# Windowed attention and a highway layer on one core: a fill in another order, earlier first completions, and a tail shared out anew between VectorE and GpSimd

## The chip, the cores and the metric

The kernel runs on one core of a Trainium2 chip. The metric is the device time of one execution in microseconds. It was 115.84 us before the change, the median of three runs from 115.61 to 115.97. PE stands for TensorE, DVE for VectorE, ACT for ScalarE, POOL for GpSimd and SP for SyncE, as in the profile.

## The reference

Attention with 4 sink keys and a window of 128 is followed by a gated layer on the result. The sizes are 4 batches, 8 heads, 768 positions, 64 elements per head, so 3072 rows of 512.

```python
scores = scale * np.matmul(q, k.transpose(0, 1, 3, 2))
keep = is_sink | in_window          # key < 4, or 0 <= query - key < 128
scores = np.where(keep, scores, -1000000000.0)
a = np.exp(scores - max); a = a / (sum + 1e-09)
x = np.matmul(a, v)                 # heads side by side: 3072 x 512
H = np.maximum(x @ w_h, 0.0)
T = 1.0 / (1.0 + np.exp(-(x @ w_t + b_t)))
out = T * H + (1.0 - T) * x
```

## The kernel before

The rows are cut into N = 24 tiles of 128 queries, NC = 6 per batch. The loop at L471 goes over steps n = 0 to 25. In step n PE computes the scores of tile n (`scores`, L265: mask matmuls L272, then L279 on the transposed q and k), the weighted values of tile n - 1 (`values`, L330, with the sink matmuls L311 and L317 of `starts` ahead of them), and the two products of the highway layer for tile n - 2 (`gate`, L369, and `hidden`, L387). Between these it transposes the attention result X of tile n - 1 (`x_transpose`, L359), which the next step's products need. In the profile a step starts with the eight L272 matmuls.

Each engine works through its own queue in the order in which the program is written; `_keep_traced_order` (L24) ties every instruction to the one ahead of it on its engine. So the order of the calls in the loop is the schedule, and lists ahead of the loop (L430 to L455) say at which step a transposition, a load or a completion comes.

**q and k** come from memory through POOL's queue, 32 partitions per load (`load_part`, L105), cast to 16 bits on the way into the tiles `nat`. DVE turns them into `tr` (`transpose_qk`, L118, the instruction L125). Batches 0 and 1 are split into three segments of 256 positions, batches 2 and 3 into two of 384. The scores of tile 3 are the first to need the third segment's q of batch 0, those of tile 4 the first to need its k. `loads` (L442) says how many loads POOL issues per step for batches 1 to 3. At most eight of POOL's loads are under way: before the next, the profile shows POOL waiting for the landing of an earlier one.

**V** comes through SP's queue (`load_v`, L129; `v_at`, L446, names the step), in steps 0 to 5 only after that step's scores. `cast_v` (L141) makes it 16 bits wide, on DVE for tiles 0 to 4 and on POOL from tile 5 on (`LATE` = 5). The outputs leave through SP's queue too, so a V load stands behind the outputs of the steps before.

**X.** ACT exponentiates the scores (`expo`, L323). When the values are in PSUM, DVE takes reciprocals of the row sums (L349) and writes X (L351): `norm`, L346. ACT copies the transposed X out of PSUM (L367) and computes tanh of the gate's product (L378, tile `TH`).

**Completion.** sigmoid(z) is 0.5 tanh(z/2) + 0.5. `diff` (L400, instruction L403) gives max(H, 0) - X in `DD`, on DVE. `complete(m)` (L423) then does three things for tile m: `gate_value` (L380, instruction L384) turns TH into 0.5 TH + 0.5, `gated` (L407, L408) multiplies DD by it on DVE, and `finish` (L411, L414) adds X and sends the sum out. Tile N - 2 takes its gate from ACT and its sum from DVE; all other sums are POOL's. Gates of tiles 12 to 20 are POOL's as well (`POOL_GATES`, L73), the others DVE's. `completed` (L449) completes tile n - 6 in step n up to step 20, and two tiles in each of the steps 21 to 24. `ahead` (L452) has the gates of tiles 15 to 20 computed on POOL earlier in the queue. The last tile is done in two halves behind the loop (L550 to L562).

DVE's queue in one step, in the middle of the run, is therefore: L349 and L351 for tile n - 1, one or two transpositions, L403 for tile n - 2, then L384 and L408 for the tile that is completed.

Of the kernel before, what the change touches and what calls it, by code (L numbers as in the profile page):

```python
# [11 lines left out]
FP32 = mybir.dt.float32  # L12
BF16 = mybir.dt.bfloat16
AF = mybir.ActivationFunctionType
ALU = mybir.AluOpType
# [22 lines left out]
def kernel(  # L38
# [13 lines left out]
    P = 128  # L52
    pe, act, dve, pool, sp = nc.tensor, nc.scalar, nc.vector, nc.gpsimd, nc.sync
# [7 lines left out]
    NT, DM = out.shape  # L61
    assert NT == B * S and DM == H * D
    NC = S // P
    N = B * NC
# [5 lines left out]
    SCALE = 1.0 / math.sqrt(D)  # L70

    LATE = 5
    POOL_GATES = range(12, 21)  # L73

    const = ctx.enter_context(tc.tile_pool(name="const", bufs=1))
    data = ctx.enter_context(tc.tile_pool(name="data", bufs=1))
    work = ctx.enter_context(tc.tile_pool(name="work", bufs=4))
# [40 lines left out]
    def transpose_qk(b, i, which, hgs=slice(0, HG)):  # L118

        t0, nt = segments[b][i]  # L120
        run = nt // 32
        src = nat[b][i][:, which, hgs].bitcast(FP32).rearrange("p hg m i -> p hg m i")
        dst = tr[b][:, which, hgs].bitcast(FP32).rearrange("p hg t e -> p hg (t e)")[
            :, :, t0:t0 + nt].rearrange("p hg (r m) -> p hg m r", m=run)
        dve.transpose(out=dst, in_=src)  # L125
# [73 lines left out]
    for g in range(1, G):  # L199
        m = away[32 * g:32 * g + 32, :]  # L200
# [5 lines left out]
                      op0=ALU.add, op1=ALU.max)  # L206
    dve.tensor_scalar(out=powers[:, 0], in0=powers[:, 0], scalar1=-1.0, scalar2=-3.0 * P,
                      op0=ALU.mult, op1=ALU.max)
    dve.tensor_scalar(out=powers[:, 1], in0=away, scalar1=-3.0, scalar2=0.0,
                      op0=ALU.add, op1=ALU.min)  # L210
    dve.tensor_scalar(out=powers[:, 2], in0=away, scalar1=0.0, scalar2=3.0,
                      op0=ALU.max, op1=ALU.min)
    dve.tensor_scalar(out=powers[:, 3], in0=powers[:, 2], scalar1=-1.0, scalar2=3.0,
                      op0=ALU.mult, op1=ALU.add)
    dve.tensor_scalar(out=inside, in0=away, scalar1=0.0, scalar2=-_OUT,
                      op0=ALU.is_ge, op1=ALU.mult)
# [127 lines left out]
    X = [None] * N  # L344

    def norm(n):  # L346
        rec = work.tile([P, HG, G], FP32, tag="rec", name="rec")
        av = ps_av[:, :, 0:G * (D + 1)].rearrange("p hg (g e) -> p hg g e", e=D + 1)
        dve.reciprocal(out=rec, in_=av[:, :, :, D])  # L349
        X[n] = work.tile([P, HG, G, D], FP16, tag="X", name="X", bufs=10)  # L350
        dve.tensor_tensor(out=X[n], in0=av[:, :, :, 0:D],  # L351
                          in1=rec.unsqueeze(3).to_broadcast([P, HG, G, D]), op=ALU.mult)
# [24 lines left out]
        TH[n] = work.tile([P, DM], FP16, tag="TH", name="TH", bufs=8)  # L377
        act.activation(out=TH[n], in_=ps_z, func=AF.Tanh, scale=0.5)  # L378

    def gate_value(n):  # L380
        if n == N - 2:
            act.activation(out=TH[n], in_=TH[n], func=AF.Copy, scale=0.5, bias=0.5)
        else:
            (pool if n in POOL_GATES else dve).tensor_scalar(  # L384
                out=TH[n], in0=TH[n], scalar1=0.5, scalar2=0.5, op0=ALU.mult, op1=ALU.add)

    def hidden(n, kcs=range(KC), cols=slice(0, DM), into=None):  # L387
# [9 lines left out]
    def flat(x, cols):  # L397
        return x.rearrange("p hg g d -> p (hg g d)")[:, cols]
# [19 lines left out]
    def idle(count):  # L418
        for _ in range(count):
            pe.matmul(ps_h, lhsT=zeros[:, 0:P], rhs=zeros, start=True, stop=True,  # L420
                      skip_group_check=True)

    def complete(m):  # L423
        if not any(m in ms for ms in ahead.values()):
            gate_value(m)
        gated(m)
        finish(m, eng=dve if m == N - 2 else pool)
# [12 lines left out]
    issues = [(b, i, g, which) for b in range(1, B) for i in range(len(segments[b]))  # L440
              for which in range(2) for g in range(G)][2 * G:]
    loads = {}  # L442
    for n, count in zip(range(2, 17), [4] * 4 + [3, 3, 3, 3, 2, 3, 3, 3, 3, 3, 3]):
        loads[n] = [issues.pop(0) for _ in range(count)]
    assert not issues
    v_at = {0: (2,), 1: (3, 4), 2: (5,), 3: (6,), 4: (7,), 5: (8,), 6: (9,), 7: (10, 11)}  # L446
    for n in range(8, N):
        v_at[n] = (n + 4,)
    completed = {n: (n - 6,) for n in range(6, 21)}  # L449
    completed.update({21: (15, 16), 22: (17, 18), 23: (19, 20), 24: (21, 22)})  # L450

    ahead = {18: (15,), 19: (16, 17), 20: (18,), 21: (19,), 22: (20,)}  # L452
    sinks_at = {2: (0, (2, 3)), 4: (0, (4, 5))}
    for b in range(1, B):
        sinks_at[b * NC + 2] = (b, (2, 3, 4, 5))  # L455
# [15 lines left out]
    for n in range(N + 2):  # L471

        nb, n1 = n - 2, n - 1
        if n < N:
            after = scores(n)
            expo(n)
            for m in v_at.get(n, ()):
                if m < N:
                    load_v(m, after if n < 6 else None)
            if n % NC == 3 and n // NC + 1 < B:  # L480
                load_sinks(n // NC + 1)
        if 4 <= n <= 6:
            hidden(n - 4 if n < 6 else 3)
        if n == 0:
            idle(5)
        starts(n1 if 0 <= n1 < N else None, nb if nb >= 0 else None)
        if 0 <= n1 < N:
            values(n1)
        if LATE <= n < N:
            cast_v(n, pool)  # L490
        if n == 2:
            sink_values(0)
            load_rows(1, 0, 0)
            load_rows(1, 0, 1)
        for b, i, g, which in loads.get(n, ()):
            load_part(b, i, g, which)
        if NC <= n < N and n % NC == 0:
            sink_values(n // NC)
        if NC <= n < N and n % NC == 1:
            sink_keys(n // NC)  # L500

        if 4 <= n <= 6:
            diff(n - 4 if n < 6 else 3)
        if n == 3:
            transpose_qk(0, 2, 1)
        turn = list(units.get(n, ()))
        if n == 5:
            transpose_qk(*turn.pop(0))
        if 0 <= n1 < N:
            norm(n1)  # L510
        if n == 1:
            transpose_qk(0, 1, 1)
        if 0 < n < LATE:
            cast_v(n, dve)
        if n == 1:
            transpose_qk(0, 2, 0)
        for unit in turn:
            transpose_qk(*unit)

        if nb >= 0:  # L520
            gate(nb)
            tanh(nb)
        if n == 5:
            hidden(2)
        if n == 1:
            idle(3)
        if 6 <= n <= N:
            hidden(nb, range(KC // 2))
        if 0 <= n1 < N:
            x_transpose(n1)  # L530
            if n in sinks_at:
                sink_scores(*sinks_at[n])
            x_copy(n1)
            if n in sinks_at:
                sink_expo(*sinks_at[n])
        if 6 <= n <= N:
            hidden(nb, range(KC // 2, KC))
        done = completed.get(n, ())
        for m in ahead.get(n, ()):
            gate_value(m)  # L540
        for m in done[:-1]:
            complete(m)
        if n == 5:
            diff(2)
        if 6 <= n <= N:
            diff(nb)
        for m in done[-1:]:
            complete(m)
# [2 lines left out]
    h_right = ps_av[:, 0, 0:DM // 2]  # L551
    hidden(last, cols=left)
    hidden(last, cols=right, into=h_right)
    O[last] = work.tile([P, DM], FP32, tag="O", name="O")
    for cols, h in ((left, None), (right, h_right)):
        diff(last, cols, h)
        dve.scalar_tensor_tensor(out=DD[last][:, cols], in0=TH[last][:, cols], scalar=1.0,
                                 in1=DD[last][:, cols], op0=ALU.add, op1=ALU.mult)
    for cols, engine in ((left, sp), (right, act)):
        dve.scalar_tensor_tensor(out=O[last][:, cols], in0=DD[last][:, cols], scalar=0.5,  # L560
                                 in1=flat(X[last], cols), op0=ALU.mult, op1=ALU.add)
        engine.dma_start(out=out[last * P:, cols], in_=O[last][:, cols])  # L562

    _keep_traced_order(tc)
# [33 lines left out]
```

## Time and profile before

| what | value |
|---|---|
| median of three runs | 115.84 us (115.61 to 115.97) |
| the profiled execution | 115.46 us, of which the span is 113.6 us |
| busy, of the span | PE 86%, PEld 46%, DVE 76%, ACT 67%, POOL 79% |
| mean granted clock of PE | 0.969 |
| chain that ended last, by engine | PE 27%, DMA 24%, DVE 19%, POOL 14% |
| DMA | 20.82 MB in 36705 packets, mean 183 GB/s |

The profile holds one execution. The span runs from the first to the last instruction; what is left up to the execution's own time lies around it. "Busy" is the time in which an engine had an instruction under way; times of instructions are given in us from the span's start. A line of the timeline gives the start, the duration, the engine and line, the tiles written and read with their shapes, and, in brackets, how long the engine had been idle and what released it. PEld are PE's weight loads, which overlap its matmuls. Matmul ends are modelled, and spans on POOL are rough.

### The profile page before, as it was taken

The page shows a single profiled execution, that of the slowest core. Times are in us where ns is not written, and L with a number is a line of the kernel's source. Part 1 is how long each engine was busy: PE and PEld are TensorE (multiplying, and loading weights), DVE is VectorE, ACT ScalarE, POOL GpSimd, SP SyncE. Part 2 cuts the span into 40 slices and gives each one's busy share as a digit, 9 for nine tenths or more (in the row PEclk, how much of TensorE's full clock was granted, in tenths as well). Part 3 has the DMA queues.
Part 4 walks back from the last instruction along what each step waited for, and adds up shares of the span by engine and source line. Part 5 has one row for each costly group of instructions (what it writes and reads, how often), then busy time and mean ns, then how long its engine had stood idle before and what let it go on. Part 6 is the DMA issues. An engine that isn't in the chain of part 4 may idle for free.

```text
span 113.6 us, 3578 instructions
## 1 busy us (share of the span) xinstructions
PE 98.3 (86%) x1414; PEld 51.8 (46%) x1414; DVE 86.2 (76%) x180; ACT 76.0 (67%) x94; POOL 90.1 (79%) x146
## 2 busy tenths in 40 slices
PE   5956773999989999999999999999979799998800
PEld 2413441644535545655465555665535366534400
DVE  6778827346394999798988978899856778899960
ACT  4476772947846588698777898785886587852500
POOL 6997549839699599999599999995989887997400
PEclk9999999769999999999999999999999999999985
DMA  3999999999999729999999999999955122424431
GB/s 87 224 234 218 175 213 247 203 218 235 187 238 151 106 71 193 253 244 223 208 247 213 198 207 243 215 197 239 287 142 151 47 85 92 185 104 179 156 149 66
DMA packets 36705, 20.82 MB, mean 183 GB/s; under 512 B 27340, under 2 KB 33232, under 8 KB 36688
## 3 DMA queue, kind: packets, MB, share of 16 engines
q1 hardware_dynamic: 29536, 13.37, 44.9%
q0 software_dynamic: 6848, 6.82, 38.0%
q10 hardware_dynamic: 304, 0.39, 1.2%
q8 instruction: 11, 0.18, 0.6%
q14 instruction: 6, 0.05, 0.2%
HBM read 21.11 MB, written 6.29 MB: 241 GB/s over the span
## 4 chain that ended last, share of the span: by engine, by line
PE 27%; DMA 24%; DVE 19%; POOL 14%; issue 7%; SPq 4%; DVEq 1%; POOLq 0%
DMA nat<-in_k_dram 7%; DMA wt<-in_moe_w_t_dram 7%; PE ps_h L390 7%; DMA wh<-in_moe_w_h_dram 7%; POOL nat L109 6%; DVE tr L125 5%; PE ps_z L371 5%; DVE DD L403 4%; DMA V<-in_v_dram 4%; PE ps_s L279 4%; DVE X L351 3%; DVE DD L408 3%; POOL TH L384 3%; PE ps_av L338 2%; SPq L174 2%
## 5 line engine op out<-in xcount | busy, mean ns | idle before, releaser
L327 ACT ACTIVATE E<-ps_s,ebias 128x2048 f16<-128x2048 f32 (+1 forms) x24 | 43.8, 1825 | 12.6 <-PE ps_s L279 12.6
L414 POOL TENSOR_TENSOR O<-DD,X 128x512 f32<-128x512 f16 x22 | 25.5, 1162 | 7.9 <-DVE DD L408 4.1
L125 DVE STREAM_TRANSPOSE tr<-nat 128x384 f32<-128x384 f32 (+1 forms) x28 | 26.1, 960 | 5.0 <-DMA nat<-in_q_dram 2.5
L390 PE MATMUL ps_h<-wh,XT 128*128 128x512 f16 (+1 forms) x96 | 27.4, 375 | 0.0
L109 POOL DMA_DIRECT2D nat<-in_k_dram x40 | 22.0, 557 | 6.1 <-DMA wt<-in_moe_w_t_dram 2.4
L371 PE MATMUL ps_z<-wt,XT 128*128 128x512 f16 x96 | 25.5, 389 | 0.0
L403 DVE SCALAR_TENSOR_TENSOR DD<-ps_h,X 128x512 f16<-128x512 f32 (+1 forms) x24 | 16.2, 674 | 8.7 <-PE ps_h L390 8.7
L378 ACT ACTIVATE TH<-ps_z 128x512 f16<-128x512 f32 x24 | 14.2, 593 | 8.4 <-PE ps_z L371 7.9
L367 ACT COPY XT<-ps_av 128x512 f16<-128x512 f16 x24 | 14.1, 586 | 6.8 <-PE ps_av L293 4.1
L109 POOL DMA_DIRECT2D nat<-in_q_dram x32 | 17.4, 551 | 1.1 <-DMA nat<-in_k_dram 1.1
L351 DVE TENSOR_TENSOR X<-ps_av,rec 128x512 f16<-128x512 f32 x24 | 16.6, 691 | 0.9
L408 DVE TENSOR_TENSOR DD<-DD,TH 128x512 f16<-128x512 f16 x23 | 13.7, 597 | 3.1 <-POOL TH L384 2.5
L279 PE MATMUL ps_s<-tr 32*128 32x256 f16 (+1 forms) x384 | 14.1, 261 | 1.9 <-DVE tr L125 1.9
L341 PE MATMUL ps_av<-v,E 128*128 128x65 f16 x192 | 14.5, 196 | 0.3 <-DVE v L142 0.2
L362 PE MATMUL ps_av<-ident,X 128*128 128x128 f16 x96 | 9.6, 224 | 4.5 <-DVE X L351 4.4
L338 PE MATMUL ps_av<-v,E 128*128 128x65 f16 x160 | 13.0, 197 | 0.0
L338 PEld LDWEIGHTS <-E 128*128 128x128 f16 x160 | 10.5, 99 | 5.5 <-issue 5.5
L341 PEld LDWEIGHTS <-E 128*128 128x128 f16 x192 | 12.1, 99 | 1.3 <-issue 1.3
L362 PEld LDWEIGHTS <-X 128*128 128x128 f16 x96 | 5.8, 99 | 14.1 <-DVE X L351 14.1
L142 POOL CAST v<-V 128x512 f16<-128x512 f32 x19 | 12.0, 632 | 0.0
L390 PEld LDWEIGHTS <-XT 128*128 128x128 f16 x100 | 8.6, 98 | 6.7 <-issue 0.4
L279 PEld LDWEIGHTS <-tr 32*128 32x128 f16 x384 | 9.2, 92 | 3.5 <-DVE tr L125 2.7
(64 smaller groups left out, 97.5 us busy)
## 6 DMA issues: line engine op xcount, KB each, us to landing
V<-in_v_dram SPq DMA_DIRECT2D x24, 256.0 KB, 5.2
out_dram<-O SPq DMA_DIRECT2D x23, 256.0 KB, 3.3
nat<-in_k_dram POOLq DMA_DIRECT2D x24, 64.0 KB, 4.4
nat<-in_q_dram POOLq DMA_DIRECT2D x16, 96.0 KB, 4.7
nat<-in_k_dram POOLq DMA_DIRECT2D x16, 96.0 KB, 4.7
nat<-in_q_dram POOLq DMA_DIRECT2D x16, 64.0 KB, 5.2
first<-in_q_dram SPq DMA_DIRECT2D x6, 128.0 KB, 3.8
wt<-in_moe_w_t_dram POOLq DMA_DIRECT2D x1, 512.0 KB, 8.0
```

The lines of the kernel that those rows point to most:

```text
L109: engine.dma_start(out=into[32 * g:32 * g + 32].rearrange("p hg m d -> p hg (m d)"), in_=(q, k)[which][b, :, t0:t0 + nt, :].rearrange("(hg ...
L125: dve.transpose(out=dst, in_=src)
L279: last = pe.matmul(ps_s[:, g, hg, 0:nq * P], lhsT=tr[b][rows, 1, hg, c * P:(c + 1) * P, e], rhs=tr[b][rows, 0, hg, c * P:(c + nq) * P, e], ...
L327: act.activation(out=E[n][:, :, :, 0:nq * P], in_=ps_s[:, :, :, 0:nq * P], func=AF.Exp, bias=ebias, scale=SCALE)
L338: pe.matmul(slot, lhsT=E[n - 1][:, g, hg, P:2 * P], rhs=v_of(n - 1)[:, h, :], start=first, stop=False, skip_group_check=True)
L341: pe.matmul(slot, lhsT=E[n][:, g, hg, 0:P], rhs=v_of(n)[:, h, :], start=first, stop=True, skip_group_check=True)
L351: dve.tensor_tensor(out=X[n], in0=av[:, :, :, 0:D], in1=rec.unsqueeze(3).to_broadcast([P, HG, G, D]), op=ALU.mult)
L371: pe.matmul(ps_z, lhsT=XT[n][:, kc * P:(kc + 1) * P], rhs=wt[:, kc, :], start=False, stop=(kc == KC - 1), skip_group_check=True)
L390: pe.matmul(into, lhsT=XT[n][:, kc * P:(kc + 1) * P], rhs=wh[:, kc, cols], start=(kc == 0), stop=(kc == KC - 1), skip_group_check=True)
L403: dve.scalar_tensor_tensor(out=DD[n][:, cols], in0=ps_h[:, cols] if h is None else h, scalar=0.0, in1=flat(X[n], cols), op0=ALU.max, op1=A ...
L408: dve.tensor_tensor(out=DD[n][:, cols], in0=DD[n][:, cols], in1=TH[n][:, cols], op=ALU.mult)
L414: eng.tensor_tensor(out=O[n][:, cols], in0=DD[n][:, cols], in1=flat(X[n], cols), op=ALU.add)
```

## The change

- **Order in steps 1 to 3.** The transpositions of batch 0's third segment move behind X (`norm`) and behind `cast_v`: q from step 1 to step 2, k within step 3.
- **V** is loaded two steps ahead in steps 0 to 5 (tiles 7 and 8 both in step 5), three steps ahead from step 6 on, where it was up to three and then four. The q and k loads of the later batches come somewhat earlier: four per step up to step 7.
- **Completions.** Tiles 0 and 1 are completed at the start of DVE's part of steps 5 and 6, instead of at the end of 6 and 7. Step 7 has none, step 14 has two, and from step 15 on tile n - 5 is completed instead of n - 6.
- **Gates.** POOL computes only those of tiles 17 and 19, in steps 21 and 22. All others but that of tile N - 2 are DVE's.
- **The end.** Tiles 16, 18, 20 and 21 (`alone`) are completed without `gate_value`, `gated` and `finish`: `twice` makes DD (TH + 1) DD, and `finish_twice` makes the output 0.5 DD + X, both on DVE. For tile 21 the second comes one step later, behind `norm` of step 24. The last tile's two halves use the same two functions, with the same instructions as before.

```diff
-    POOL_GATES = range(12, 21)
...
-    def gate_value(n):
+    def gate_value(n, engine=dve):
...
-            (pool if n in POOL_GATES else dve).tensor_scalar(
+            engine.tensor_scalar(
                 out=TH[n], in0=TH[n], scalar1=0.5, scalar2=0.5, op0=ALU.mult, op1=ALU.add)
...
+    def twice(n, cols=slice(0, DM)):
+        dve.scalar_tensor_tensor(out=DD[n][:, cols], in0=TH[n][:, cols], scalar=1.0,
+                                 in1=DD[n][:, cols], op0=ALU.add, op1=ALU.mult)
+
+    def finish_twice(n, cols=slice(0, DM), queue=sp):
+        if O[n] is None:
+            O[n] = work.tile([P, DM], FP32, tag="O", name="O")
+        dve.scalar_tensor_tensor(out=O[n][:, cols], in0=DD[n][:, cols], scalar=0.5,
+                                 in1=flat(X[n], cols), op0=ALU.mult, op1=ALU.add)
+        queue.dma_start(out=out[n * P:(n + 1) * P, cols], in_=O[n][:, cols])
+
     def complete(m):
-        if not any(m in ms for ms in ahead.values()):
+        if m in alone:
+            twice(m)
+            if m != N - 3:
+                finish_twice(m)
+            return
+        if m not in ahead.values():
             gate_value(m)
         gated(m)
         finish(m, eng=dve if m == N - 2 else pool)
...
-    for n, count in zip(range(2, 17), [4] * 4 + [3, 3, 3, 3, 2, 3, 3, 3, 3, 3, 3]):
+    for n, count in zip(range(2, 17), [4] * 6 + [3, 3, 3, 3, 3, 3, 2, 2, 2]):
         loads[n] = [issues.pop(0) for _ in range(count)]
...
-    v_at = {0: (2,), 1: (3, 4), 2: (5,), 3: (6,), 4: (7,), 5: (8,), 6: (9,), 7: (10, 11)}
-    for n in range(8, N):
-        v_at[n] = (n + 4,)
-    completed = {n: (n - 6,) for n in range(6, 21)}
-    completed.update({21: (15, 16), 22: (17, 18), 23: (19, 20), 24: (21, 22)})
-
-    ahead = {18: (15,), 19: (16, 17), 20: (18,), 21: (19,), 22: (20,)}
+    v_at = {n: (n + 2,) for n in range(6)}
+    v_at[5] = (7, 8)
+    for n in range(6, N):
+        v_at[n] = (n + 3,)
+    completed = {5: (0,), 6: (1,), 14: (8, 9)}
+    completed.update({n: (n - 6,) for n in range(8, 14)})
+    completed.update({n: (n - 5,) for n in range(15, 21)})
+    completed.update({21: (16, 17), 22: (18, 19), 23: (20, 21), 24: (22,)})
+
+    alone = (16, 18, 20, 21)
+    ahead = {21: 17, 22: 19}
...
+        done = list(completed.get(n, ()))
+        if 5 <= n <= 6:
+            complete(done.pop(0))
         if 4 <= n <= 6:
             diff(n - 4 if n < 6 else 3)
-        if n == 3:
-            transpose_qk(0, 2, 1)
...
             norm(n1)
+        if n == N:
+            finish_twice(N - 3)
...
             cast_v(n, dve)
-        if n == 1:
-            transpose_qk(0, 2, 0)
+        if n in (2, 3):
+            transpose_qk(0, 2, n - 2)
...
-        for m in ahead.get(n, ()):
-            gate_value(m)
+        if n in ahead:
+            gate_value(ahead[n], pool)
         for m in done[:-1]:
             complete(m)
```

More of the change, by code (lines that the diff above doesn't have):

```diff
@@ L537 @@
             hidden(nb, range(KC // 2, KC))
-        done = completed.get(n, ())
-        for m in ahead.get(n, ()):
-            gate_value(m)
+        if n in ahead:
+            gate_value(ahead[n], pool)
         for m in done[:-1]:
```

10 lines of the change are left out of this document (3 added, 7 removed).

## The prediction

> **What bounds the kernel now.** I read the page's engine shares first: PE is busy 86% of 113.6 us, so time lies in its gaps and in what the steps take over their PE work. The timeline of PE gives the step starts (the L272 matmuls): 14.01, 19.89, 24.36, 28.95, 33.32, 38.41 for steps 2 to 7, later one every 3.2 to 4.0 us. Then I compared steps of one position in their batch, by the windows view; columns are length, busy us of PE, its weight loads, DVE, ACT, POOL, the granted clock, DMA share and GB/s.
> ```profile
> 60.27:63.64 3.37, 3.37 (x47) 1.72 (x47) 3.13 (x7) 2.75 (x4) 3.35 (x5) 1.00 0.98 211
> 63.64:67.64 4.00, 4.00 (x87) 2.28 (x87) 3.42 (x7) 3.33 (x5) 3.99 (x8) 1.00 0.94 206
> 81.70:85.86 4.16, 3.49 (x48) 1.73 (x48) 2.75 (x6) 3.10 (x4) 3.62 (x5) 1.00 0.55 146
> 85.86:90.82 4.96, 4.16 (x87) 2.24 (x87) 3.17 (x6) 3.10 (x4) 4.42 (x9) 1.00 0.40 106
> ```
> Steps 13 and 14 are full (PE busy throughout: 3.37, 4.00). Steps 19 and 20 do the same work in 4.16 and 4.96. The DVE timeline says why:
> ```profile
> 83.77 0.42 DVE L408 TENSOR_TENSOR DD<-DD,TH 128x512 f16<-128x512 f16 x1 [1.19 <-POOL TH L384]
> 88.27 0.42 DVE L408 TENSOR_TENSOR DD<-DD,TH 128x512 f16<-128x512 f16 x1 [1.27 <-POOL TH L384]
> ```
> DVE stands in front of the product L408 until POOL has halved the gate; the next X (L349, L351) is behind it, and PE waits for X at 85.09 and 89.60. The fill, step 2, has another queue of this kind:
> ```profile
> 17.31 1.10 DVE L125 STREAM_TRANSPOSE tr<-nat 128x512 f32<-128x512 f32 x1 [2.53 <-DMA nat<-in_q_dram]
> 18.26 0.15 DVE L349 RECIPROCAL rec<-ps_av 128x8 f32<-128x8 f32 x1
> ...
> 19.21 0.40 PE L362 MATMUL ps_av<-ident,X 128*128 128x128 f16 x4 [1.75 <-DVE X L351]
> ```
> The values matmuls were done at 16.6, yet X waits behind a transposition that waits for q. Last the tail, DVE and POOL side by side:
> ```profile
> 96.49 0.69 DVE L351 TENSOR_TENSOR X<-ps_av,rec 128x512 f16<-128x512 f32 x1
> ...
> 100.28 1.36 DVE L408 TENSOR_TENSOR DD<-DD,TH 128x512 f16<-128x512 f16 x1
> 101.57 0.68 DVE L403 SCALAR_TENSOR_TENSOR DD<-ps_h,X 128x512 f16<-128x512 f32 x1
> 102.17 1.34 DVE L408 TENSOR_TENSOR DD<-DD,TH 128x512 f16<-128x512 f16 x1
> ```
> ```profile
> 98.94 2.42 POOL L414 TENSOR_TENSOR O<-DD,X 128x512 f32<-128x512 f16 x2
> 101.31 0.81 POOL L142 CAST v<-V 128x512 f16<-128x512 f32 x1
> 102.08 1.15 POOL L414 TENSOR_TENSOR O<-DD,X 128x512 f32<-128x512 f16 x1
> ```
> L408 alone takes 0.43; here it ends only 0.3 to 0.4 after the POOL instruction under way has ended, and the cast behind it grows from 0.61 to 0.81. DVE and POOL exclude each other for this instruction. So X of tile 23 starts (L349) at 103.43, though its values were done at 102.8, and DVE reaches the last tile at 107.62.
>
> **The change part by part**, against the profiled execution: 115.46 us, of which 113.6 is the span; that is 0.38 below the median of the three runs, 115.84.
>
> 1. **X ahead of the transpositions, steps 2 and 3.** L349 moves from 18.26 to 16.7, X is done at 17.63, its transposition on PE starts at 17.68, not 19.21. But scores(3) need q of segment three, and DVE now does cast_v(2) before that transposition. The trace's landing events put V2 at 18.42 (the cast of before, at 19.08, did not wait). Cast 18.47 to 18.89, transposition 18.83 to 19.93 (1.10): scores(3) at 19.98, before 20.12. The sinks' exponentials are early now, so L317 no longer waits 0.3 for them: values(2) at 20.77, not 21.23. The k transposition, formerly run in DVE's idle time at 21.60, comes after X(2) and cast_v(3): values end 21.5, X to 22.4, cast to 22.8, transposition 22.7 to 23.8. Scores(4) 23.9, before 24.67 (on PE, gate(1) at the half clock that the windows view shows from 21.15 to 24.56 leads to the same 23.9). **-0.76**, and steps 4 to 6 move along: wh landed at 24.27, hidden(0) now wants it at 24.46; the batch-1 k landed at 29.62, wanted at 32.1. Bounds: 0, and -1.5 if V2 comes a microsecond sooner.
> 2. **V one step later, loads earlier.** V4 is asked for at 15.3 instead of 12.4, V5 at 20.5 instead of 15.3; that is 12 and 11 us ahead of their casts, and landings took 4.1 to 8.7 us in the view of the tile V (by the landing events V5 alone took 12.3). In the steady part V is 9 to 10 us ahead instead of 12 to 14. On SP's queue the output of tile 0 now stands ahead of V9, which goes from 29.97 to some 36.7, and that of tile 1 ahead of V10, as late as before (41.6); their casts come at 47 and later. Nothing waits: 0. POOL's q and k loads get up to one V of traffic out of the way before 24 us (256 KB at the 205 GB/s that the windows view gives for step 3 is 1.3 us); I count half of it, 0.6 us, on POOL's queue only.
> 3. **Tiles 0 and 1 completed in steps 5 and 6**, in DVE idle of 1.92 and 1.18 us (before L403): 0.7 each (L384 0.28, L408 0.43) is hidden. Step 7 loses this 0.7 behind two transpositions: there the L349 came at 43.92 though the values were done at 43.4. Step 8 after it took 4.42 against 4.00 for step 14: **-0.42**. On POOL, two sums (1.10 each), two more loads (0.54 each) and the rest put sk (L253) at 44.75 less 0.6, that is 44.15; PE then wants it at 45.23 - 0.76 - 0.42 = 44.05. **+0.1**, between 0 and 0.7.
> 4. **Step 14 completes two tiles.** On DVE the extra 0.7 fits the 0.69 idle before 67.81. On POOL one sum more, one load less: 1.10 - 0.54 = 0.56 on cast_v(15), which had 0.48 to spare (end 71.73, needed 72.21): **+0.1**. From step 15 POOL has less to do than before.
> 5. **The gates back on DVE.** No wait for POOL in steps 18 to 20. DVE then does what it did in steps 12 to 14. Steps 19 and 20 go to 3.37 and 4.00: 0.79 + 0.96 = **-1.75**.
> 6. **The end.** DVE gets `twice` and `finish_twice` for tiles 16, 18, 20, 21; POOL keeps the sums of 17 and 19 and their gates. Durations: 0.69 each by L403 (same operation and size; L557 at half the size is 0.42, L403 at half size 0.42). The second reads what the first wrote, so it starts 0.05 after the first's end instead of 0.08 before. Do they, like L408, wait for POOL? Both their inputs lie in SBUF, as L408's do. L351 is a TENSOR_TENSOR too, but with one input in PSUM, and at 96.49 kept its 0.69 beside POOL's sum; L403 did at 101.57. So the operands decide in this trace, not the operation, and I take the L408 rows. With before's clock lined up at step 21 (90.82): L349 92.58, X to 93.43, `twice` 93.43 to 94.1 (POOL's sum of 15 ends at 93.4), POOL's cast 94.1 to 94.65, `finish_twice` to 95.33, L403 beside POOL's gate (0.58) to 95.9, L408 to 96.3. The next L349 is at 96.30 (before 96.26). Step 22 in the same way, with 0.3 of waiting for the sum of 17: 100.32 (99.43). Step 23, with no POOL gate but two more operations of DVE: 104.64 (103.43). Then 21's finish, L403, ACT's gate of 22, L408 and L414: the last tile at 108.3, before 107.62. **+0.7**. If they don't exclude POOL, the same chain gives 99.3, 102.85 and 106.48: -1.1.
>
> The Trainium skill (SBUF — State Buffer, "Who interferes with whom") says that a DVE instruction with two SBUF inputs contends with a GpSimd instruction that reads SBUF, and that who started first keeps the other out for the whole instruction. It speaks against part 6; the L408 rows agree, and no row has a SCALAR_TENSOR_TENSOR of that kind beside POOL. By the rule the part is +0.7, without it -1.1.
>
> Sum: -0.76 - 0.42 + 0.1 + 0.1 - 1.75 + 0.7 = -2.03: 113.4 for the profiled execution, 113.8 for the median.
>
> **Rivals.**
> - No exclusion in the tail. For: the operation is another than L408's. Against: the operands. -0.76 - 0.42 + 0.2 - 1.75 - 1.1 = -3.83: 112.0.
> - POOL gets in first. At 93.43 DVE and POOL's cast ask at the same moment; if the cast wins in each tail step, every step waits some 0.5 longer: L349 at 96.8, 101.4, 105.8, the last tile at 109.4, +1.8 in place of +0.7: 114.9. Against it: the waiting L408 won over the cast at 101.31.
> - The fill gives nothing, since what X gains is lost waiting for q and k transposed behind it: part 1 is 0, 114.6.
> - Slower: in step 2 cast_v(2) now stands on DVE ahead of the q transposition, and nothing of PE's covers it. Scores(3) start 1.56 after V2's landing, and all after it moves one for one. V2 took 9.3 us from its issue at 9.13. At 20.45 (11.3 us) the whole gain is gone. By the landing events V5 took 12.3 us; V2 as slow as that lands at 21.4, +3.0: 116.8. For: the DMA engines are full there. Against: V3, right behind it in the queue, landed at 19.5, and nothing ahead of V2 changes.
>
> **How the numbers follow.** Forecast 113.8 with 0.48, no exclusion 112.0 with 0.20, POOL first 114.9 with 0.13, nothing from the fill 114.6 with 0.11, V2 late 116.8 with 0.05; 0.03 for a mixture near no change. The range takes all but the last two, with 0.2 to 0.3 for the small terms' bounds: 111.7 to 115.1. A measurement of this kernel tells about 0.3% (0.35 us) from no change: faster 0.90 (the four gains less 0.02 for their spread), within 0.04, slower 0.06.
>
> **What would show it.** Right: scores(4) 0.6 to 0.9 earlier; no L408 waiting for POOL TH in steps 18 to 20, and these steps at 3.4 and 4.0; in the tail `twice` or `finish_twice` above 0.9 us where a POOL instruction runs, and steps 22 to 24 longer than before. Wrong: `twice` at 0.69 beside POOL's sum (then 112); scores(3) waiting beyond 20.1 for the transposition; PE waiting for sk in step 8.

## The result, and the profile after

The changed kernel takes 115.12 us (median of 20 runs, 114.20 to 116.04), the kernel before 115.91 (20 runs beside them): a ratio of 0.9935, 95% interval 0.9906 to 0.9965, some 0.75 us gained. The forecast was 113.8 with a range from 111.7 to 115.1. The direction is right; of the 2.03 us about a third came, and the median lies 0.02 above the range. Ratios here leave out runs more than 1.5% above the fastest of their kernel, medians don't; this matters most for one kernel, three edits (below), where three of six runs are left out.

The profiled execution of after took 114.20 us, span 112.2; it is among the fastest of its 20 runs, so what is good in it may be better than usual. Line numbers of after are one less than before's up to the tail: L403 is now L402, L408 L407, L384 L383, L349 L348; L423 is `twice`, L429 `finish_twice`. First the windows view of after, for steps 14, 15, 19 and 20 (columns: length, busy us of PE, its weight loads, DVE, ACT, POOL, granted clock, DMA share, GB/s).

```profile
62.53:66.53 4.00, 4.00 (x86) 2.27 (x86) 3.93 (x8) 3.34 (x5) 3.98 (x8) 1.00 0.92 207
66.53:71.88 5.35, 3.71 (x56) 2.04 (x56) 5.20 (x8) 3.24 (x5) 4.57 (x7) 1.00 1.01 229
82.43:85.73 3.30, 3.30 (x46) 1.74 (x45) 3.05 (x7) 2.68 (x3) 2.49 (x3) 1.00 0.67 177
85.73:89.73 4.00, 4.00 (x86) 2.28 (x85) 3.41 (x7) 3.41 (x5) 2.28 (x5) 1.00 0.50 135
```

Steps 19 and 20 are 3.30 and 4.00 (before 4.16 and 4.96): PE is busy in all of both, as forecast. Step 15 is new: 5.35, before 3.53, with DVE busy for 5.20 of it. The DVE timeline shows that the product no longer waits for POOL in the late steps; there is no bracket on the line of step 19 (nor on that of step 20, at 87.10):

```profile
83.53 0.43 DVE L407 TENSOR_TENSOR DD<-DD,TH 128x512 f16<-128x512 f16 x1
```

Where the 1.82 of step 15 went stands in the timeline of DVE, from the completions that step 14 issues to the next X, and of POOL in the same stretch:

```profile
65.86 1.03 DVE L383 TENSOR_SCALAR TH<-TH 128x512 f16<-128x512 f16 x1
66.93 0.71 DVE L407 TENSOR_TENSOR DD<-DD,TH 128x512 f16<-128x512 f16 x1
67.56 0.68 DVE L402 SCALAR_TENSOR_TENSOR DD<-ps_h,X 128x512 f16<-128x512 f32 x1
68.16 1.60 DVE L383 TENSOR_SCALAR TH<-TH 128x512 f16<-128x512 f16 x1
69.80 0.42 DVE L407 TENSOR_TENSOR DD<-DD,TH 128x512 f16<-128x512 f16 x1
70.14 0.20 DVE L348 RECIPROCAL rec<-ps_av 128x8 f32<-128x8 f32 x1
```
```profile
65.58 1.15 POOL L413 TENSOR_TENSOR O<-DD,X 128x512 f32<-128x512 f16 x1
66.69 0.67 POOL L141 CAST v<-V 128x512 f16<-128x512 f32 x1
67.31 1.11 POOL L108 DMA_DIRECT2D nat<-in_q_dram  x2
68.43 1.16 POOL L413 TENSOR_TENSOR O<-DD,X 128x512 f32<-128x512 f16 x1
```

The gate L383 takes 0.28 alone. Here the first ends 0.16 after POOL's sum of tile 7, the second 0.17 after the sum of tile 8 (68.43 to 69.59). X of tile 14 starts at 70.14, its values done near 68.2, and PE stands for 1.64 us ahead of the transposition (L361, at 71.12).

In the fill, the three engines' lines that answer to those of before:

```profile
16.22 0.21 DVE L348 RECIPROCAL rec<-ps_av 128x8 f32<-128x8 f32 x1 [1.34 <-PE ps_av L340]
...
17.17 0.86 DVE L141 CAST v<-V 128x512 f16<-128x512 f32 x1
17.95 1.09 DVE L124 STREAM_TRANSPOSE tr<-nat 128x512 f32<-128x512 f32 x1
```
```profile
17.21 0.40 PE L361 MATMUL ps_av<-ident,X 128*128 128x128 f16 x4 [0.24 <-DVE X L350]
...
19.09 0.64 PE L278 MATMUL ps_s<-tr 32*128 32x256 f16 x16 [0.80 <-DVE tr L124]
```

X waits for nothing but its values, and PE's wait for X is 0.24, not 1.75. Scores(3) wait for the transposed q instead, to 19.09. V2 had landed at 17.14 in this execution. Last the tail, DVE and POOL side by side:

```profile
95.89 0.95 DVE L423 SCALAR_TENSOR_TENSOR DD<-TH,DD 128x512 f16<-128x512 f16 x1
96.86 0.98 DVE L429 SCALAR_TENSOR_TENSOR O<-DD,X 128x512 f32<-128x512 f16 x1
...
102.29 0.69 DVE L423 SCALAR_TENSOR_TENSOR DD<-TH,DD 128x512 f16<-128x512 f16 x1
```
```profile
95.13 1.15 POOL L413 TENSOR_TENSOR O<-DD,X 128x512 f32<-128x512 f16 x1 [0.54 <-DVE DD L407]
96.23 1.08 POOL L141 CAST v<-V 128x512 f16<-128x512 f32 x1
97.27 1.05 POOL L383 TENSOR_SCALAR TH<-TH 128x512 f16<-128x512 f16 x1
```

`twice` and `finish_twice` take 0.95 and 0.98 beside POOL and 0.69 and 0.68 (102.29 and 103.74) once POOL has nothing to do. POOL pays as well: its cast takes 1.08 and its gate 1.05 (some 0.61 each alone).

Step by step, after against before in the two profiled executions: start of step 5 27.50 against 28.95 (1.45 gained), step 8 4.76 against 4.42 (0.34 lost), step 15 1.82 lost, steps 19 and 20 1.82 gained, from step 21 to the last tile's first L402 16.89 against 16.80 (0.09 lost), and 0.46 gained behind that, from the issue of the last output on. Together some 1.5, the difference of the spans (113.64 and 112.18).

### The profile page after: what moved, and what is told of

It reads as the page before. It is cut to its first block, busy times and chain, and to the rows that moved or that the text cites. A ratio compares the mean times of both kernels' runs of the same rounds, so it can differ in the third digit from the quotient of the medians.

```text
span 112.2 us, 3574 instructions
## 1 busy us (share of the span) xinstructions
PE 97.4 (87%) x1414; PEld 51.4 (46%) x1414; DVE 90.4 (81%) x187; ACT 75.7 (68%) x94; POOL 83.2 (74%) x135
## 5 line engine op out<-in xcount | busy, mean ns | idle before, releaser
L413 POOL TENSOR_TENSOR O<-DD,X 128x512 f32<-128x512 f16 x18 | 20.8, 1153 | 10.4 <-issue 7.1
L370 PE MATMUL ps_z<-wt,XT 128*128 128x512 f16 x96 | 24.6, 379 | 0.0
L402 DVE SCALAR_TENSOR_TENSOR DD<-ps_h,X 128x512 f16<-128x512 f32 (+1 forms) x24 | 16.1, 673 | 7.0 <-PE ps_h L389 6.8
L340 PE MATMUL ps_av<-v,E 128*128 128x65 f16 x192 | 14.1, 193 | 0.6 <-DVE v L141 0.6
L141 POOL CAST v<-V 128x512 f16<-128x512 f32 x19 | 13.0, 686 | 0.0
L361 PE MATMUL ps_av<-ident,X 128*128 128x128 f16 x96 | 9.4, 220 | 3.9 <-DVE X L350 3.8
L337 PE MATMUL ps_av<-v,E 128*128 128x65 f16 x160 | 12.7, 194 | 0.0
L340 PEld LDWEIGHTS <-E 128*128 128x128 f16 x192 | 11.8, 97 | 1.8 <-issue 1.8
L337 PEld LDWEIGHTS <-E 128*128 128x128 f16 x160 | 10.2, 97 | 4.9 <-issue 4.8
L389 PEld LDWEIGHTS <-XT 128*128 128x128 f16 x100 | 8.7, 98 | 6.8 <-issue 0.6
L361 PEld LDWEIGHTS <-X 128*128 128x128 f16 x96 | 5.7, 97 | 12.9 <-DVE X L350 12.9
L370 PEld LDWEIGHTS <-XT 128*128 128x128 f16 x96 | 7.8, 98 | 6.0 <-ACT XT L366 0.3
```

Source lines behind the costliest of these rows:

```text
L337: pe.matmul(slot, lhsT=E[n - 1][:, g, hg, P:2 * P], rhs=v_of(n - 1)[:, h, :], start=first, stop=False, skip_group_check=True)
L340: pe.matmul(slot, lhsT=E[n][:, g, hg, 0:P], rhs=v_of(n)[:, h, :], start=first, stop=True, skip_group_check=True)
L361: pe.transpose(xt[:, kc // 2, (kc % 2) * P:(kc % 2 + 1) * P], x[:, kc * P:(kc + 1) * P], ident)
L370: pe.matmul(ps_z, lhsT=XT[n][:, kc * P:(kc + 1) * P], rhs=wt[:, kc, :], start=False, stop=(kc == KC - 1), skip_group_check=True)
L389: pe.matmul(into, lhsT=XT[n][:, kc * P:(kc + 1) * P], rhs=wh[:, kc, cols], start=(kc == 0), stop=(kc == KC - 1), skip_group_check=True)
L402: dve.scalar_tensor_tensor(out=DD[n][:, cols], in0=ps_h[:, cols] if h is None else h, scalar=0.0, in1=flat(X[n], cols), op0=ALU.max, op1=A ...
```

## The experiments

All were timed in five rounds beside the kernel before, whose medians there were 115.76 to 115.91. The times are medians; the ratio is to before.

| kernel | us | ratio, 95% interval | step 5 begins | step 8 | step 15 | steps 19, 20 |
|---|---|---|---|---|---|---|
| before (profiled) | 115.91 | 1 | 28.95 | 4.42 | 3.53 | 4.16, 4.96 |
| after (profiled) | 115.12 | 0.9935 (0.9906 to 0.9965) | 27.50 | 4.76 | 5.35 | 3.30, 4.00 |
| one completion each | 114.02 | 0.9810 (0.9767 to 0.9852) | 28.58 | 4.42 | 3.53 | 3.31, 3.99 |
| sums swapped | 114.51 | 0.9851 (0.9809 to 0.9894) | 29.09 | 4.01 | 4.15 | 3.30, 3.99 |
| sink keys first | 114.98 | 0.9910 (0.9877 to 0.9943) | 28.87 | 4.02 | 5.42 | 3.31, 3.99 |
| fill only | 115.51 | 0.9949 (0.9916 to 0.9981) | 29.12 | 4.41 | 3.53 | 4.15, 4.96 |
| cast behind | 114.96 | 0.9937 (0.9896 to 0.9978) | 31.17 | 4.01 | 5.39 | 3.30, 4.00 |
| gates only | 115.33 | 0.9967 (0.9935 to 0.9999) | 30.03 | 4.42 | 3.53 | 3.30, 4.00 |
| none alone | 115.77 | 0.9984 (0.9952 to 1.0015) | 32.02 | 4.01 | 5.36 | 3.30, 4.00 |
| three edits | 114.02 | 0.9738 (0.9671 to 0.9804) | 29.17 | 4.41 | 3.54 | 3.31, 4.00 |
| hidden(0) later | 113.13 | 0.9765 (0.9719 to 0.9811) | 26.59 | 5.07 | 3.53 | 3.30, 4.00 |
| old fill | 113.86 | 0.9839 (0.9780 to 0.9898) | 29.28 | 4.42 | 3.54 | 3.31, 4.00 |
| new fill again | 113.83 | 0.9818 (0.9763 to 0.9873) | 29.25 | 4.56 | 3.54 | 3.31, 3.99 |
| loads later | 111.89 | 0.9695 (0.9640 to 0.9751) | 26.28 | 4.97 | 3.53 | 3.30, 4.00 |

The step columns come from one profiled execution each. Those of "cast behind" (117.14 us) and "none alone" (118.55) are 2% above their medians, and their loss lies ahead of step 5, where both show a granted clock of 0.50 for some 4 us (26 to 30 and 22 to 26).

**One completion each.** Step 14 has one completion like every step; from step 5 on, step n completes tile n - 5, so step 7 has one again.

```diff
-    completed = {5: (0,), 6: (1,), 14: (8, 9)}
-    completed.update({n: (n - 6,) for n in range(8, 14)})
-    completed.update({n: (n - 5,) for n in range(15, 21)})
+    completed = {n: (n - 5,) for n in range(5, 21)}
```

> The changed kernel, but tile n - 5 is completed in every step from 5 to 20: tile 2 in step 7, and step 14 has one tile instead of two. Theory A (the two tiles of step 14 hold up DVE, so that step 15 is 5.35 us instead of 3.53): step 15 at 3.5 to 3.6, step 8 at 4.4 to 4.8 (tile 2 now stands in step 7 behind two transpositions, but PE waits there for the sink keys anyway), and the time 1.4 to 1.8 us below the changed kernel, a ratio to before of 0.978 to 0.982. Rival R (POOL, not DVE, is what is late there): POOL's work in steps 8 to 14 is the same to within one sum, so the wait comes back in a neighbouring step and the ratio stays at 0.992 to 0.995.

The time falls by 1.1 us against after, to a ratio of 0.9810. The window of step 15, and the gate that step 14 issues, behind L402:

```profile
68.28:71.81 3.53, 3.53 (x56) 2.05 (x56) 2.99 (x6) 3.07 (x5) 3.51 (x7) 1.00 1.04 228
```
```profile
68.45 0.69 DVE L402 SCALAR_TENSOR_TENSOR DD<-ps_h,X 128x512 f16<-128x512 f32 x1 [0.68 <-PE ps_h L389]
69.06 0.28 DVE L383 TENSOR_SCALAR TH<-TH 128x512 f16<-128x512 f16 x1
```

PE is busy throughout step 15 again. With one completion DVE's gate comes behind L402, at 69.06, after POOL's sum and cast (which end at 69.04), and takes 0.28. Step 7's stall is back (step 8 4.42), and yet the kernel is 1% faster: the two completions of step 14 are the loss.

**Sums swapped.** Both completions stay in step 14, but POOL's sum of tile 8 is asked for only after DVE's gate of tile 9.

```diff
         for m in done[:-1]:
-            complete(m)
+            if n == 14:
+                gate_value(m)
+                gated(m)
+            else:
+                complete(m)
...
         for m in done[-1:]:
             complete(m)
+            if n == 14:
+                finish(done[0])
```

> The changed kernel with two tiles in step 14, but POOL adds tile 9 before tile 8, so that no sum is under way when DVE comes to the second gate. Same instructions on every engine. Theory A1 (DVE and POOL exclude each other: the second gate took 1.60 us because POOL's loads and then its sum of tile 8 ran): the second gate (L383) at 0.3 to 0.7, step 15 at 4.2 to 4.5 instead of 5.35, the time some 1.0 us lower, ratio 0.983 to 0.987. Theory A2 (DVE simply has 0.7 us too much to do in step 14): step 15 stays at 5.2 to 5.4 and the ratio at 0.992 to 0.995.

Step 15 falls to 4.15. The gates of DVE, and POOL:

```profile
67.22 1.04 DVE L383 TENSOR_SCALAR TH<-TH 128x512 f16<-128x512 f16 x1
...
69.53 0.38 DVE L383 TENSOR_SCALAR TH<-TH 128x512 f16<-128x512 f16 x1
```
```profile
66.94 1.16 POOL L413 TENSOR_TENSOR O<-DD,X 128x512 f32<-128x512 f16 x1
...
70.51 2.27 POOL L413 TENSOR_TENSOR O<-DD,X 128x512 f32<-128x512 f16 x2 [0.72 <-issue]
```

The work is the same, one sum comes later, and the second gate takes 0.38, not 1.60. Step 15 alone overstates what that wins: step 16 takes 3.85, not 3.54, since POOL's cast of V now stands behind two sums in one piece (it starts at 72.73) and PE waits for it. Over both steps the swap takes back 0.89 of the 1.82. So about half of the loss is shown to be the exclusion of the second gate, and not the mere number of DVE's instructions. The rest goes with the first gate, which still starts under the sum of tile 7 and takes 1.04, and its product (0.71 for 0.43); that they are the other half is read from these lines, and no run takes the first gate alone out of POOL's way.

**Sink keys first.** In steps 7, 13 and 19 sk is made ahead of the loads on POOL's queue (after).

```diff
+        if NC <= n < N and n % NC == 1:
+            sink_keys(n // NC)
         for b, i, g, which in loads.get(n, ()):
             load_part(b, i, g, which)
...
-        if NC <= n < N and n % NC == 1:
-            sink_keys(n // NC)
```

> The changed kernel, but in steps 7, 13 and 19 POOL makes the sink keys (sk) before it issues the step's loads instead of behind them. Theory S (step 8 is 4.76 us instead of 4.00 because PE waits for sk behind four loads): L292 of step 8 no longer waits for POOL, step 8 at 4.0 to 4.1, the time 0.6 to 0.8 us lower, ratio 0.986 to 0.989. Rival: DVE or the exponentials set step 8 anyway, or POOL's cast is what is late next; step 8 stays above 4.5 and the ratio at 0.992 to 0.995.

Step 8 is 4.02 as theory S hoped, sk at 42.53 and wanted at 44.74. But the time is that of after within the intervals, and the ratio lies between the two forecasts. The likely reason is in the table: "sums swapped" has 4.01 without the edit, since PE reached step 8 later there (42.36, in after 40.26). Of all the profiles only after's, whose fill ran fast, has PE waiting for sk in step 8.

**Fill only.** The kernel before with the new order of the transpositions, of V and of the loads.

```diff
-    for n, count in zip(range(2, 17), [4] * 4 + [3, 3, 3, 3, 2, 3, 3, 3, 3, 3, 3]):
+    for n, count in zip(range(2, 17), [4] * 6 + [3, 3, 3, 3, 3, 3, 2, 2, 2]):
...
-    v_at = {0: (2,), 1: (3, 4), 2: (5,), 3: (6,), 4: (7,), 5: (8,), 6: (9,), 7: (10, 11)}
-    for n in range(8, N):
-        v_at[n] = (n + 4,)
+    v_at = {n: (n + 2,) for n in range(6)}
+    v_at[5] = (7, 8)
+    for n in range(6, N):
+        v_at[n] = (n + 3,)
...
-        if n == 3:
-            transpose_qk(0, 2, 1)
...
-        if n == 1:
-            transpose_qk(0, 2, 0)
+        if n in (2, 3):
+            transpose_qk(0, 2, n - 2)
```

> The kernel before with the fill's edits alone: X ahead of the third segment's transpositions, V two and later three steps ahead, the loads earlier; completions, gates and tail as before. Theory F (the fill is worth what the two traces show, 1.45 us at the start of step 5, and keeps it): steps 2 to 4 together 13.5 us instead of 14.9, the lead at step 9 0.7 to 1.4 us (step 7's completion and the sink keys behind one more load take some of it), steps 19 and 20 as before at 4.2 and 5.0; ratio 0.988 to 0.994. Rival: the lead is lost to POOL, whose casts are nearly late in steps 12 to 15, and the ratio is 0.998 to 1.002.

It gains 0.5% (0.2 to 0.8), less than theory F and more than its rival, yet in its profile step 5 begins at 29.12, not before 28.95. DVE's timeline has what takes the place of X's wait:

```profile
17.50 0.69 DVE L351 TENSOR_TENSOR X<-ps_av,rec 128x512 f16<-128x512 f32 x1
19.38 0.50 DVE L142 CAST v<-V 128x512 f16<-128x512 f32 x1 [1.20 <-DMA V<-in_v_dram]
19.81 1.07 DVE L125 STREAM_TRANSPOSE tr<-nat 128x512 f32<-128x512 f32 x1
```

X is early, then DVE stands 1.20 for V2, with the transposition that scores(3) need behind it. This is the mechanism of the rival "slower", at a smaller price. "One completion each", "sums swapped" and "sink keys first" have the same wait (0.89, 1.39, 1.15); after, with V2 at 17.14, has none.

**Cast behind.** In after, `cast_v` in steps 2 and 3 goes behind the transposition of the third segment, so V2 holds nothing up.

```diff
-        if 0 < n < LATE:
-            cast_v(n, dve)
         if n in (2, 3):
             transpose_qk(0, 2, n - 2)
+        if 0 < n < LATE:
+            cast_v(n, dve)
```

> The changed kernel, but in steps 2 and 3 cast_v stands behind the transposition of the third segment instead of ahead of it on DVE. Theory V (in step 2 DVE waits for V2 with the q transposition behind it: 0.9 to 1.4 us in four of the five profiles with this fill, none in the one that ran fastest): no DVE wait for V ahead of the q transposition, scores(3) start 0.8 to 1.4 us sooner after X of tile 1 than in those four (X done to L279 of step 3 at 1.2 to 1.4 us instead of 2.3 to 2.9), the time 0.5 to 1.0 us below the changed kernel, ratio 0.985 to 0.990. Rival W (the fill is set by the landings of wh and of k behind it, and what scores(3) gain is waited for again at hidden(0) in step 4): scores(3) earlier, but L390 of step 4 no earlier, ratio 0.991 to 0.995.

No change in time (0.9937 against 0.9935), as rival W has it. Steps 3 and 4 begin early (18.41 and 21.82), but then PE stands at `hidden(0)` until wh has landed, 1.14 us. That is the smaller part of what this profile loses in step 4, which takes 9.35 us with the half clock in it. But the kernel with three edits, which keeps this one, has the same wait at a granted clock of 1.00 (below).

**Gates only.** The kernel before, with all gates but that of tile N - 2 on DVE, and nothing else.

```diff
-    POOL_GATES = range(12, 21)
+    POOL_GATES = ()
...
-    ahead = {18: (15,), 19: (16, 17), 20: (18,), 21: (19,), 22: (20,)}
+    ahead = {}
```

> The kernel before with one edit: every gate that POOL computed is DVE's (no POOL_GATES, none ahead); fill, completions and sums as before. Theory G (steps 19 and 20 are long because DVE waits for POOL's gates): steps 19 and 20 at 3.3 to 3.4 and 4.0, 1.7 to 1.8 us together; in the tail DVE has one more gate per tile, each beside POOL's sums, so from step 21 to the last tile's L403 it takes 16.8 to 17.6 instead of 16.80; ratio 0.984 to 0.991. Rival: DVE is full in step 19 (3.5 us of work) and the wait comes back as a late X; steps 19 and 20 stay above 8.4 together, ratio 0.995 to 1.002.

Steps 19 and 20 become 3.30 and 4.00, the whole 1.82 of part 5, as theory G said. But the time is in the rival's range, and the kernel gains 0.4 us of it: from step 21 to the last tile's first L403 it takes 17.93 us, before 16.80. DVE's gates in the tail show why:

```profile
94.49 0.83 DVE L384 TENSOR_SCALAR TH<-TH 128x512 f16<-128x512 f16 x1
...
98.49 0.92 DVE L384 TENSOR_SCALAR TH<-TH 128x512 f16<-128x512 f16 x1
```

They stand beside POOL's sums (94.01 to 95.17, 98.10 to 99.26) and end 0.15 after them. The gates gain where POOL leaves room between its instructions, and lose where two tiles are completed in a step.

**None alone.** After, with the tiles of the tail by gate, product and POOL's sum; the gates of tiles 17 and 19 stay POOL's.

```diff
-    alone = (16, 18, 20, 21)
+    alone = ()
...
-        if n == N:
-            finish_twice(N - 3)
```

> The changed kernel without the part at the end: tiles 16, 18, 20 and 21 get gate and product from DVE and the sum from POOL like the others. Theory L (every operation of DVE's with both inputs in SBUF excludes POOL, twice and finish_twice too, which took 0.75 to 1.03 us beside POOL and 0.69 alone, so moving sums to DVE buys little): from the start of step 21 to the last tile's L403 16.7 to 17.3 us instead of 16.89, the time within 0.4 us of the changed kernel. Rival (the sums on DVE are what relieves the tail): 17.6 us or more, 0.7 us above the changed kernel, ratio 0.999 or more.

0.9984 against after's 0.9935: by the ratios the tail by DVE alone is worth 0.5%, but their intervals overlap. In the profile the same stretch takes 17.30, after 16.89, which is near the upper end of theory L; the medians are 0.65 us apart, which is nearer to the rival's 0.7. So part 6 is no gain over the tail of before, but one of 0.4 to 1.0 us over the two tails (17.30 here, 17.93 in "gates only") that are left without it once the gates are DVE's.

**Three edits.** The diffs of "one completion each", "sink keys first" and "cast behind" together.

> The changed kernel with three edits together: one completion in each step from 5 to 20, sink keys ahead of the loads, cast_v behind the transpositions in steps 2 and 3. If the three costs add up: step 15 at 3.53 (1.8 saved), scores(3) 0.8 to 1.4 sooner in most runs, step 8 at 4.4 (tile 2's completion in step 7 now sets it, the sink keys no longer do): ratio 0.972 to 0.977. If the fill is set by landings after all: 0.980 to 0.983, as with one completion in each step alone.

The median is 114.02, as with one edit; the ratio is 0.9738, as if the three costs added up, but its interval overlaps that of 0.9810. Whether they add up is not shown. PE's timeline in step 4, which takes 6.36:

```profile
25.46 1.02 PE L389 MATMUL ps_h<-wh,XT 128*128 128x512 f16 x4 [1.33 <-DMA wh<-in_moe_w_h_dram]
```

**hidden(0) later.** The three edits, and in step 4 `hidden(0)` goes behind `gate(2)` on PE, `diff(0)` to the end of the step on DVE.

```diff
-        if 4 <= n <= 6:
+        if 5 <= n <= 6:
             hidden(n - 4 if n < 6 else 3)
...
-        if 4 <= n <= 6:
+        if 5 <= n <= 6:
             diff(n - 4 if n < 6 else 3)
...
-        if n == 5:
-            hidden(2)
+        if 4 <= n <= 5:
+            hidden(0 if n == 4 else 2)
...
-        if n == 5:
-            diff(2)
+        if 4 <= n <= 5:
+            diff(0 if n == 4 else 2)
```

> The kernel with the three edits (one completion per step, sink keys ahead of the loads, cast behind the transposition), and in step 4 hidden(0) on PE behind gate(2), diff(0) on DVE at the step's end. Two theories of what the fill still loses. W: in step 4 PE stands in front of hidden(0) until wh lands (1.1 and 1.3 us in the two profiles of kernels with the cast moved), with values(3) queued behind it. Then the wait is gone or under 0.3, step 4 is 0.6 to 1.2 shorter, and the time is 0.3 to 1.0 per cent under that of the kernel with three edits (ratio to before 0.964 to 0.971). K: what is behind the wait on PE waits for something as late (the cast of V, the k transposition with its load); then the wait reappears at values(3), X(3) or the scores of step 5, and the ratio stays at 0.974 within 0.003.

Step 4 is 4.36 and step 5 begins at 26.59, the wait is gone. Not all of the 2.00 us that step 4 is shorter by is the edit's: wh landed at 23.98 in this execution and at 25.41 in that of "three edits". Of the 2.58 us by which step 5 begins earlier than there, only 1.25 is left when step 10 begins (48.63 against 49.88): PE now waits for POOL's cast of V in step 8, and again in step 9 (0.52, at 46.13).

```profile
41.45 0.19 PE L340 MATMUL ps_av<-v,E 128*128 128x65 f16 x1 [0.89 <-POOL v L141]
```

The wait for wh went as W said, and the ratio stayed where K put it, though not for K's reason: the queue that took half of the gain stands four steps later. By the medians the time fell by 0.9 us; by the ratios, whose intervals overlap, this is not settled.

**Old fill and new fill again.** "One completion each" with the fill of before (the diff of "fill only" backwards), beside a second copy of it with the new one (no edit).

> The changed kernel with one completion per step and with the fill of before (transpositions of the third segment ahead of X in steps 1 and 3, V up to four steps ahead, later loads). F1: the new fill is worth what the kernel of before gained from it alone, 0.5 per cent: ratio 0.984 to 0.988, start of step 5 some 0.3 to 1 us later than with the new fill in the same call. F2: the forecast's 0.76 us: ratio 0.987 to 0.989. F0: the fill is worth nothing, since V2, wh and k set its end: ratio 0.979 to 0.983, the same as the run beside it.

> The changed kernel with one completion per step once more, beside the one with the old fill. Its ratio should come again at 0.981 (0.977 to 0.985), step 15 at 3.5. F1 expects it 0.3 to 0.7 per cent under the old fill, F2 0.6 to 0.8, F0 level with it.

113.86 and 113.83, ratios 0.9839 and 0.9818: the second copy repeats the first one's 0.9810, and the pair differs by 0.03 us in the medians and by 0.2% in the ratios, with intervals of 0.6% to either side. F0, F1 and F2 are not told apart by this pair; with the 0.5% of "fill only" (0.2 to 0.8), a worth of the fill from nothing to some 1.0 us is left open.

**Loads later.** "hidden(0) later" with POOL's loads four per step only up to step 5.

```diff
-    for n, count in zip(range(2, 17), [4] * 6 + [3, 3, 3, 3, 3, 3, 2, 2, 2]):
+    for n, count in zip(range(2, 18), [4] * 4 + [3] * 8 + [2] * 4):
```

> The kernel with the three edits and hidden(0) later, with POOL's loads spread otherwise: four per step to step 5, three from step 6 to 13, two from 14 to 17 (48 as before). In the profile of its forerunner, step 5 began at 26.59, some 2.5 us ahead of the other kernels with this fill, but steps 8 and 9 took 5.07 and 4.22 in place of 4.42 and 3.54, with PE waiting 0.89 and 0.52 for POOL's cast of V. P: in a fast fill POOL's queue, of which the loads are half, is what bounds steps 6 to 9. Then one load less (0.54) in each of steps 6 and 7 takes 1.0 to 1.4 us from steps 8 and 9 where the fill is as fast; where it is slow, nothing is won; the time is 0 to 0.9 per cent under that of its forerunner (ratio to before 0.968 to 0.977). L: the loads moved later land too late for the transpositions of steps 8 and 9, or for those of the last batch (steps 15 to 20); then a transposition waits for DMA there and the ratio is 0.977 to 0.985.

111.89 us, 0.9695: the fastest of all, 3.0% under the kernel before, and 0.7% under its forerunner by the ratios, whose intervals just overlap. Step 9 falls from 4.22 to 3.63, step 8 keeps 0.80 of the wait for the cast and 4.97. Step 10 begins at 47.85 against 48.63, and behind it the two run alike. P's price was 1.0 to 1.4 on steps 8 and 9; 0.7 came. No transposition waits for a late load, so L is out.

## Why the prediction was right and wrong

**The step that failed is the fourth.** "On DVE the extra 0.7 fits the 0.69 idle" counted DVE's work by its times alone and looked on POOL only at the queue. It measured +1.82 in place of +0.1. The prediction had read in the tail of before that L408 and POOL exclude each other, and had used it in its sixth step; it did not ask the same of the two gates and two products that step 14 places beside a POOL busy for 3.99 of 4.00 us in the prediction's own row, nor that `finish` of the first tile hands POOL a sum that then keeps out the gate of the second. "One completion each" shows the price of the second tile, "sums swapped" that half of it is the second gate's wait for POOL.

A row of before already had such a gate. DVE's only one beside a sum of POOL's, in the tail, took 0.62 where 0.28 is usual, and ended 0.15 after that sum:

```profile
104.27 0.62 DVE L384 TENSOR_SCALAR TH<-TH 128x512 f16<-128x512 f16 x1
```
```profile
103.59 1.15 POOL L414 TENSOR_TENSOR O<-DD,X 128x512 f32<-128x512 f16 x1 [0.36 <-DVE DD L408]
```

The Trainium skill (SBUF — State Buffer, "Who interferes with whom") says that `tensor_scalar` too, and not only an instruction with two SBUF inputs, can contend with GpSimd, since it can enter two-port modes, in which DVE takes the pair of ports that the two share. The trace agrees: 1.03 and 1.60 for a gate of 0.28.

**The sum without it.** "One completion each" has neither part 4 nor step 7's gain. Without these two terms (+0.1 and -0.42) the forecast is 114.1, a ratio of 0.985; it measures 114.02 and 113.83, 0.9810 and 0.9818. That this is near is in part luck, since two other steps did not come as written, and their errors point in opposite directions:

- **Part 1, -0.76.** X was early in every profile of the new fill, scores(4) even at 22.97 in after's, but the size stays open: 0.2 to 1.0 us by "fill only", 0.03 by the medians of the pair. The step took V2's landing of one execution, 18.42. In the profiles that keep the cast ahead of the transposition, DVE does not wait for V2 in one (after), waits 0.89 to 1.39 in five and 2.82 in one ("none alone"); each such wait goes into scores(3). And if V2 holds nothing up, wh does ("cast behind", "three edits"). The profiled execution's 1.45 is one in which both came early. The rival "the fill gives nothing" is not refuted as a size, but its reason (q and k transposed behind X) is not what the profiles show: what lay behind was a load.
- **Part 6, +0.7.** The exclusion is there: 0.75 to 1.03 beside POOL, 0.69 without. But the whole stretch cost 0.09. I had L349 of the tail 3.72, 4.02 and 4.32 apart; it came 3.53, 3.67 and 4.20 apart (91.50, 95.03, 98.70, 102.90), 0.66 less in sum. DVE and POOL took turns, and POOL's cast and gate, 1.08 and 1.05 in place of 0.61, carried their share of the waiting.

**Part 3, -0.42 and +0.1 for sk.** The stall behind step 7 goes: step 8 is 4.01 where PE comes late. In after's profile, where PE comes early, POOL takes 0.75 back: some 0.55 by sk, inside the bound of 0.7 that the step gave, and 0.2 by its cast of V. That the early completions are hidden held in after's profile, but not in all. In three of the eleven profiles with them the gate or the product of tile 1 ran into POOL's sum of tile 0, and step 6 took 6.00, 5.57 and 5.61 ("one completion each", "sums swapped", "new fill again") instead of 5.09. It is the error of the fourth step once more, here in "one completion each":

```profile
34.02 1.93 DVE L383 TENSOR_SCALAR TH<-TH 128x512 f16<-128x512 f16 x1
```
```profile
34.62 1.17 POOL L413 TENSOR_TENSOR O<-DD,X 128x512 f32<-128x512 f16 x1
```

**Part 5, -1.75,** measured -1.82. **Part 2, 0:** no wait for a later V in the steady steps; but the loads brought forward to steps 6 and 7, which I had priced by their traffic alone, stand ahead of POOL's casts of V, and PE waits for these once it gets there early ("loads later").

**The rivals.** "No exclusion" is refuted by the 0.95 and 0.98. "POOL first" is what happened, in step 14 and not in the tail; that the loss of one step equals the price it named for the whole tail (1.8) is chance. The range was too narrow because each price of the exclusion was asked for the tail alone.

## What to carry to other kernels

Where two engines exclude each other for an instruction, idle time of the one is room for it only where the other is idle too; before an instruction is moved, read both timelines at its new place, and ask what its result sets free on the other engine. A fill is judged over several executions, since one profile shows one landing of each load. And after each wait that is removed, look for the load or the queue that is next: here V2, wh, POOL's casts, one behind the other, and only the kernel that eases all three ("loads later") is clearly faster than "one completion each".

## What the runs showed that I had not expected

- A waiting DVE instruction is not always next. In after the second gate was under way from 68.16, beside POOL's loads to 68.42, and POOL's sum went in at 68.43 ahead of it; before, the waiting L408 had won over the cast at 101.31.
- POOL's issuing of a load does not always hold DVE's gate out. A gate that fell into the first half of a load took 0.28 (69.06 in "one completion each", the load from 68.99). One that met a load's end took 0.38 and ended 0.12 after it (69.53 in "sums swapped", the loads to 69.79). In after the second gate met the end of a load and then the sum. The gate of 1.93 began 0.06 before the end of a load, was not done during the next one (34.07 to 34.61), and ended 0.16 after the sum behind it. It is read from a few lines and was not tried by itself, and whether a gate gets in beside a load stays open.
- In after's fill DVE's cast L141 took 0.86, beside POOL's sink values (16.64 to 17.74), where 0.43 is usual.
- The same fill begins step 5 at 27.50 to 29.12 in the profiles of after, "one completion each", "sums swapped", "sink keys first" and "fill only". The half clock that before shows from 21.15 to 24.56 comes at another time, or not at all, in other executions: the mean granted clock is 0.57 from 21 to 25 in "sums swapped", 0.57 from 16 to 20 in "one completion each", and 1.00 from 21 to 25 in "old fill" and after.
